# A fused attention and feed-forward kernel on one core: the pooled weights' product on both row halves, a new planned order, and more matmuls ahead of the first transpose

## The chip, the cores and the metric

The kernel runs on 1 core of one Trainium2 chip. The metric is the device time of one execution in microseconds; lower is better. The kernel before took 918.63 us, the median of 3 runs (918.45 to 920.07).

Names of the engines: PE (TensorE, matmuls), DVE (VectorE), ACT (ScalarE), POOL (GpSimd) and SP, whose queue issues nearly all the transfers. PEld is PE's loading of weights.

## The reference, cut to what matters

```
q, k, v: 8 batches x 8 heads x 576 rows x 64         (fp32)
pooled:  rows averaged in fours -> 144 rows; softmax(q4 k4^T / 8) v4; each result row repeated 4 times
local:   softmax of q k^T / 8 where |i - j| < 4, times v
x = (pooled + local) as 4608 tokens x 512
h = x @ w_in                       (512 x 2048)
g = h * clip(h + 3, 0, 6) / 6
out = g @ w_out                    (2048 x 512)
```

All of it is fp32. The two large products are made of three matmuls each on values split in a high and a low part (hi*hi, hi*lo, lo*hi).

## The kernel before, in words

**Feed-forward.** The 4608 tokens are 9 chunks of 512 (PART). A chunk has 16 steps f. Step f of the first product (`gemm1`, line 1031) is 12 matmuls of 128x512 into PSUM bank h0 or h1. Then ACT makes relu(h+3) (line 1037), DVE min(.,6)*h (line 1041), ACT the high part (line 1045), and DVE or POOL the low part (line 1049). Step f of the second product (`gemm2`, line 1081) is 12 matmuls into the four banks o0 to o3, one for each 128 tokens. All in all that is 2 x 1728 matmuls of this kind.

**Attention.** A unit is two heads of one batch, 32 units in all. The first 8 units (`alone`, batches 0 and 1) have their steps planned one by one: q and k are transposed by PE (line 385, batch 0), masks (699) and local scores (707), pooled scores (504), softmax on DVE, ACT and POOL, transposes of the probabilities (597, 732), and the products with v (`pv_d` 678, `pv` 750). The other 24 units go in bursts: one PE operation holds the pooled scores of a new unit (`scores_d4`, 521), the products of an older unit (`pv`, 750, and `pv_d4`, 666), and the local scores of the new one (707). A burst works in banks h0 and h1. The transposed probabilities of these units come by way of DRAM (`put_d`, `get_d`, `put`, `get`).

**The pooled product of a burst.** `pv_d4` multiplies 144 pooled probabilities by the pooled v. 128 of the 144 rows are on 128 partitions, two row halves of 64. The last 16 rows of the two heads are 32 partitions of the lower row half. So there are three passes: row half 0, row half 1, and row half 0 once more for the rest, with 144 columns each and two heads side by side.

**Weights.** Each block of `w_in` or `w_out` comes as 64-bit numbers and is made into two fp32 parts: ACT (line 185), "low" on ACT or DVE (198, 200), "bits" on DVE (190), "hi" on ACT or DVE (119, 121: a helper, `copy_on`) and "lo" on POOL or DVE (210).

**What sets the order.** The program makes a list of operations with a cost each, what they depend on, the buffers they take and a due time. `Plan.emit` walks through time with these costs and picks for each free engine the operation that is due first. T0, TC, TF and FIRST are due times, COST and PEN the costs and preferences where more than one engine can do an operation, `dma` and `Queue` the model of the transfers. An operation with `lock` on DVE or POOL is not put beside another one of that kind on the other of the two. While PE has nothing to do before the first gemm, `busy` (line 1133) puts matmuls on the identity between its operations. The result is a fixed list of instructions for each engine; on the chip each engine works through its own list in order and waits only for its operands.

## Time and profile before

| | |
|---|---|
| median of 3 runs | 918.63 us (918.45 to 920.07) |
| profiled execution, own time | 915.05 us |
| its span, first to last instruction | 913.2 us |
| PE busy | 899.2 us (98%), 7002 matmuls |
| DVE, ACT, POOL busy | 530.9 us (58%), 430.1 us (47%), 230.2 us (25%) |
| mean granted TensorE clock | 0.999 |
| moved by DMA | 93.41 MB, 102 GB/s over the span |

The profiled execution was 3.58 us shorter than the median of the runs, and its span 1.85 us shorter than its own time. A matmul's recorded time overlaps with that of the next one, so the pace of PE is read from the starts of its rows, not from a mean. In a row of the order of time the columns are: start in us, length in us, engine, line, operation, result and operand, tile of the array or shapes, number of instructions, and in brackets the idle time before it with what ended it.

### The profile page before, as it was taken

Reading aid. Unit: us, or ns where it says so; the run is one execution under the profiler, and the core shown is the slowest. Engines: PE = TensorE matmul, PEld = TensorE weight load, DVE = VectorE, ACT = ScalarE, POOL = GpSimd, SP = SyncE. Lnnn points to the kernel's source line nnn. Section 1 sums busy time; section 2 is a strip of 40 time slices with the busy share of each in tenths; the row PEclk is TensorE's granted clock in tenths of the full one; section 3 lists DMA queues with packets and bytes.
Section 4 is the critical chain, followed back from the end, with each engine's and each line's share of the span. In section 5 each row is a group of like instructions: output and inputs, shape, how many; then the busy total and the mean of one; then the engine's idle time right before and its main releaser. Section 6 shows DMA issues by size and latency. Waiting matters only on the chain.

```text
span 913.2 us, 19160 instructions
## 1 busy us (share of the span) xinstructions
PE 899.2 (98%) x7002; PEld 730.9 (80%) x7002; DVE 530.9 (58%) x965; ACT 430.1 (47%) x1438; POOL 230.2 (25%) x316
## 2 busy tenths in 40 slices
PE   8899999999999999999999999999999999999997
PEld 6577778788888888888888888888888888888886
DVE  7989866676755567556745675556654432233222
ACT  5977745566554555345535564455542222222221
POOL 5685532222322231223212330225000000010000
PEclk9999999999999999999999999999999999999999
DMA  9989433666736456355644555555522010001001
GB/s 251 290 231 293 100 82 77 128 120 134 146 85 128 100 112 144 78 104 106 139 97 93 114 116 126 105 104 105 134 59 48 1 47 1 1 1 46 1 1 46
DMA packets 311565, 93.41 MB, mean 102 GB/s; under 512 B 250800, under 2 KB 296880, under 8 KB 311472
## 3 DMA queue, kind: packets, MB, share of 16 engines
q1 hardware_dynamic: 310800, 91.29, 44.4%
q8 instruction: 55, 0.90, 0.4%
q10 hardware_dynamic: 672, 0.91, 0.3%
q14 instruction: 38, 0.31, 0.1%
HBM read 69.53 MB, written 22.61 MB: 101 GB/s over the span
## 4 chain that ended last, share of the span: by engine, by line
PE 91%; DVE 3%; DMA 2%; ACT 1%; SPq 1%; issue 1%; POOL 0%; ACTq 0%; DVEq 0%
PE h L1031 42%; PE o L1081 41%; PE a L707 2%; PE h L750 1%; PE h L666 1%; PE a L521 1%; DMA arena<-in_k_dram 1%; ACT arena L571 1%; DMA out_dram<-arena 0%; DMA pd<-arena 0%; PE a L504 0%; PE a L678 0%; SPq L985 0%; DMA arena<-in_v_dram 0%; PE a L750 0%
## 5 line engine op out<-in xcount | busy, mean ns | idle before, releaser
L1081 PE MATMUL o<-wp,rounded 128*128 128x512 f32 x1728 | 414.4, 392 | 0.0
L1031 PE MATMUL h<-rounded,wp 128*128 128x512 f32 x1728 | 407.8, 391 | 2.0 <-DVE first L755 1.4
L1031 PEld LDWEIGHTS h<-rounded,wp 128*128 128x128 f32 x1728 | 322.6, 188 | 72.0 <-issue 2.8
L1081 PEld LDWEIGHTS o<-wp,rounded 128*128 128x128 f32 x1728 | 321.2, 188 | 69.4 <-issue 0.8
L1041 DVE SCALAR_TENSOR_TENSOR arena<-arena,h 128x512 f32<-128x512 f32 x144 | 97.8, 679 | 127.1 <-ACT arena L1037 126.8
L1037 ACT ACTIVATE arena<-h 128x512 f32<-128x512 f32 x144 | 85.7, 595 | 181.7 <-PE h L1031 180.8
L1045 ACT CAST rounded<-arena 128x512 fp32r<-128x512 f32 x144 | 88.8, 617 | 112.1 <-DVE arena L1041 61.9
L1049 DVE TENSOR_TENSOR rounded<-arena,rounded 128x512 fp32r<-128x512 f32 x105 | 72.4, 692 | 101.5 <-PE o L1081 96.6
L1049 POOL TENSOR_TENSOR rounded<-arena,rounded 128x512 fp32r<-128x512 f32 x39 | 51.9, 1333 | 168.5 <-PE o L1081 88.7
L377 DVE STREAM_TRANSPOSE arena<-arena 128x576 f32<-128x576 f32 x56 | 43.3, 775 | 67.3 <-DMA arena<-in_q_dram 34.1
L571 ACT ACTIVATE arena<-arena 128x64 f32<-128x64 f32 x240 | 80.1, 336 | 0.2
L571 ACT ACTIVATION_READ_ACCUMULATOR arena<-arena 128x1 f32 x240 | 45.3, 189 | 0.0
L453 POOL TENSOR_TENSOR arena<-arena 32x256 f32<-32x256 f32 (+1 forms) x26 | 19.4, 746 | 94.4 <-DMA arena<-in_v_dram 90.7
L547 ACT ACTIVATE arena<-arena 128x1 f32<-128x1 f32 (+1 forms) x78 | 15.0, 192 | 47.6 <-DVE arena L560 47.6
L454 POOL TENSOR_TENSOR arena<-arena 32x128 f32<-32x128 f32 (+1 forms) x26 | 12.8, 494 | 96.9 <-PE h L666 95.7
L682 ACT ACTIVATE arena<-h 128x144 f32<-128x144 f32 x24 | 7.0, 290 | 63.7 <-PE h L666 63.7
L451 DVE TENSOR_REDUCE arena<-arena 128x128 f32<-128x512 f32 (+1 forms) x26 | 27.6, 1061 | 13.4 <-PE h L666 9.2
L934 POOL TENSOR_TENSOR rounded<-arena,rounded 128x768 fp32r<-128x768 f32 (+3 forms) x5 | 8.9, 1789 | 98.4 <-ACT rounded L119 94.8
L415 POOL TENSOR_TENSOR arena<-arena 128x144 f32<-128x144 f32 x52 | 31.8, 612 | 4.1
L588 DVE TENSOR_TENSOR arena<-arena 128x432 f32<-128x432 f32 (+1 forms) x42 | 29.8, 710 | 1.4
L633 DVE STREAM_TRANSPOSE arena<-arena 128x384 f32<-128x384 f32 (+1 forms) x48 | 22.2, 467 | 13.5 <-DMA arena<-pd 13.0
L707 PE MATMUL a<-arena 64*64 64x64 f32 x1160 | 28.7, 224 | 0.0
(192 smaller groups left out, 783.9 us busy)
## 6 DMA issues: line engine op xcount, KB each, us to landing
arena<-in_v_dram SPq DMA_DIRECT2D x58, 160.0 KB
rawp<-in_w_in_dram SPq DMA_DIRECT2D x16, 512.0 KB
rawp<-in_w_out_dram SPq DMA_DIRECT2D x16, 512.0 KB
arena<-in_q_dram SPq DMA_DIRECT2D x112, 72.0 KB
arena<-in_k_dram SPq DMA_DIRECT2D x112, 72.0 KB
pl<-arena SPq DMA_DIRECT2D x24, 320.0 KB
arena<-pl SPq DMA_DIRECT2D x96, 80.0 KB
arena<-in_v_dram SPq DMA_DIRECT2D x28, 256.0 KB
```

The lines of the kernel that those rows point to most:

```text
L377: nc.vector.transpose(out=qk[kind], in_=qk[kind])
L415: eng.tensor_tensor(t, t, x[:, :, r], op=ALU.add)
L451: eng.tensor_reduce(out=vd, in_=raw.rearrange("p r e -> p e r"), op=ALU.add, axis=AX.X)
L571: nc.scalar.activation(x[:, j], x[:, j], AF.Exp, bias=m[:, j:j + 1], scale=0.125, accum_out=s[:, j:j + 1])
L588: eng.tensor_tensor(x, x, s.unsqueeze(2).broadcast_to(list(x.shape)), op=ALU.mult)
L707: nc.tensor.matmul(st["ps", g][half:half + WIN, jj * D:jj * D + WIN], qk_of("q")[hs, k_first:k_first + WIN], qk_of("k")[hs, k_first:k_firs ...
L1031: nc.tensor.matmul(st["ps"], win[f][:, wt, kk * P:(kk + 1) * P], xs[part][:, kk], start=(kk == 0 and i == 0), stop=(kk == NK - 1 and i == ...
L1037: nc.scalar.activation(st["t"], st["ps"], AF.Relu, bias=3.0)
L1041: nc.vector.scalar_tensor_tensor(out=t, in0=t, scalar=6.0, in1=st["ps"], op0=ALU.min, op1=ALU.mult)
L1045: nc.scalar.copy(st["gh"], st["t"])
L1049: eng.tensor_tensor(st["gl"], st["t"], st["gh"].bitcast(F32), op=ALU.subtract)
L1081: nc.tensor.matmul(otile[n, m], gt[:, ms], wout[f][:, wt], start=(f == 0 and i == 0), stop=(f == NF - 1 and i == 2),)
```

## The change

- `pv_d4`: the last 16 rows of both heads are put on both row halves of the array, on partitions 0 to 31 and 64 to 95. Row half 0 then makes the first 24 of the 48 query columns of each group, and row half 1 the last 24. `ld4`, `sum4`, `get_d` and `turn_d` put the operands there: four small loads of v in place of two, one more memset, and transposes and multiplications of 96 partitions in place of 32.
- The planner's numbers: due times (T0 from 55.0 to 44.6, FIRST, LAGW, a list SHIFT of one offset for each unit), costs of transfers (`dma`, LAND, SLOW, LATE), costs and preferences of engines (COST, PEN), a doubled PE cost before COLD = 5.9, and a rule (`sooner`) by which an operation waits for another engine that would finish it earlier.
- The high part of g (`ghi`) may be made by DVE as well as by ACT. It, the split of x (`xhi`) and, where it is not done by way of a PSUM bank, the "hi" of the weights are locked against POOL.
- More matmuls on the identity are put ahead of the first transpose, by another rule in `fetch`.
- The last chunk: steps f = 14 of two of the four banks are done ahead of f = 15, each bank is evicted by one engine (ACT or DVE) in place of two halves one after the other, and the stores are dealt to SP and ACT by size.

```
@@ pv_d4
-            for g in (0, 1, 2):
-                ks = slice(g % 2 * D, (g % 2 + 1) * D)
+            for g in range(2):
+                ks = slice(g * D, (g + 1) * D)
                 for h in range(2):
                     hs = slice(h * D, (h + 1) * D)
                     nc.tensor.matmul(
-                        st["pod"][g % 2][hs].rearrange("p (j q) -> p j q", j=3), st["vd"][ks, g // 2, hs],
-                        used(st["pdt"][ks], h * D, 2 * D) if g < 2 else used(st["pdt"][ks], 6 * D, D),
-                        start=(g < 2), stop=(g > 0), skip_group_check=True)
+                        st["pod"][g][hs].rearrange("p (j q) -> p j q", j=3), st["vd"][ks, 0, hs],
+                        used(st["pdt"][ks], *((3 * h * D, D) if apart else (h * D, 2 * D))), start=True, stop=False,
+                        skip_group_check=True)
+            for g in range(2):
+                ks, q = slice(g * D, (g + 1) * D), QB // 2
+                x = st["pdt"][ks]
+                for h in range(2):
+                    hs = slice(h * D, (h + 1) * D)
+                    nc.tensor.matmul(
+                        st["pod"][g][hs].rearrange("p (j q) -> p j q", j=3)[:, :, g * q:(g + 1) * q], st["vd"][ks, 1, hs],
+                        bass.AP(tensor=x.tensor, offset=x.offset + 6 * D + g * NAR, ap=[x.ap[0], [D, 3], [1, q]]),
+                        start=False, stop=True, skip_group_check=True)
@@ ld4
-                for h in range(2):
-                    nc.sync.dma_start(
-                        raw[h * KR:(h + 1) * KR], src(v_all, row0 + 4 * P, [[4 * ROW, KR], [1, 4 * ROW]]))
+                for first in (0, KR, D, D + KR):
+                    nc.sync.dma_start(raw[first:first + KR], src(v_all, row0 + 4 * P, [[4 * ROW, KR], [1, 4 * ROW]]))
@@ sum4
-                eng.memset(st["vd"][NAR:D, 1], 0.0)
+                for i in range(2):
+                    eng.memset(st["vd"][i * D + NAR:(i + 1) * D, 1], 0.0)
@@ turn_d
-            n, a, e = (P, 0, 12 * NAR) if i == 0 else (NAR, 12 * NAR, 18 * NAR)
+            n, a, e = (P, 0, 12 * NAR) if i == 0 else (D + NAR, 12 * NAR, 18 * NAR)
@@ plan_weights, plan_split, plan_moe
-        e = op(on("whi", cols), 0, hi, [d])
+        e = op(on("whi", cols), 0, hi, [d], lock=not by_bank)
...
-                       free=free, dl=start_of(n) - 1.0)
+                       free=free, dl=start_of(n) - 1.0, lock=True)
...
-            d = op("ACT", 0.17 + size / 1130, hi, [c], take=[("gh" + k0, ("gh", key))])
+            d = op(on("ghi", size), 0, hi, [c], take=[("gh" + k0, ("gh", key))], lock=True)
@@ plan_store (last chunk)
-            e = [op("ACT", 0.37, partial(ev_half, 0, nc.scalar), [ready], take=[("obz", (n, m))], free=[frees])]
-            e.append(op("DVE", 0.37, partial(ev_half, 1, nc.vector), [ready] + e, take=[("obz", (n, m))], free=[frees]))
+            e = [op("ACT" if m % 2 == 0 else "DVE", (0.60, 0.69)[m % 2], partial(ev_last, nc.scalar if m % 2 == 0 else nc.vector), [ready],
+                    take=[("obz", (n, m))], free=[frees])]
@@ numbers
-T0, TC, TF, LAG = 55.0, 82.0, 5.1, 2
+T0, TC, TF, LAG = 44.6, 82.0, 5.1, 2
-FIRST = 16.0, 8.0
+FIRST = 7.5, 4.1
-    "whi": {"ACT": (0.12, 1 / 1200), "DVE": (0.1, 1 / 960)},
+    "whi": {"ACT": (0.12, 1 / 1200), "DVE": (0.09, 1 / 1800)},
+    "ghi": {"ACT": (0.17, 1 / 1130), "DVE": (0.09, 1 / 1800)},
-    return Load(packets * (7.8 + 0.0446 * size if size > 256 else 10.8 + 0.0375 * size) / 16e3, packets / 16)
+    return Load(packets * (18.0 + 0.045 * size if size > 256 else 10.8 + 0.0375 * size) / 16e3, packets / 16)
@@ fetch
-            self.idle = self.warm.start + 1.2
+            self.idle = self.warm.start + 0.4
...
-            gap = (t - self.idle - IDLE[1]) * (IDLE[2] if t > 8.0 else 0.5 * IDLE[2])
-            o.busy = max(0, int(gap / IDLE[0]))
+            one = IDLE[0] if t > COLD else 2 * IDLE[0]
+            gap = (t - self.idle - IDLE[1]) * (IDLE[2] if t > COLD else 1.0)
+            o.busy = max(0, int(gap / one))
```

Three places of the order. The first is PE's list at its very start; `identb` is the identity, `h` the bank the fill writes, `a` and `o` banks that take transposes, scores follow. Before, 3 matmuls on the identity stand ahead of the first transpose:

```order
L1133 MATMUL h_114<-identb 128x512
L385 MATMUL a_118<-ident,arena 128x128 x4
L385 MATMUL a_125<-ident,arena 128x128 x4
L385 MATMUL o_132<-ident,arena 128x128
L385 MATMUL o_134<-ident,arena 128x128
L385 MATMUL o_145<-ident,arena 128x128 x4
L699 LDWEIGHTS identb
L699 MATMUL o_153<-maskb,identb 128x320
```

and now 14, with one more before the second unit's transposes:

```order
L1151 MATMUL h_117<-identb 128x512
L387 MATMUL a_132<-ident,arena 128x128 x4
L387 MATMUL a_139<-ident,arena 128x128 x4
L387 MATMUL o_146<-ident,arena 128x128
L387 MATMUL o_148<-ident,arena 128x128
L1151 LDWEIGHTS identb
L1151 MATMUL h_117<-identb 128x512
L387 MATMUL o_158<-ident,arena 128x128 x4
L710 LDWEIGHTS identb
L710 MATMUL o_164<-maskb,identb 128x320
```

What follows is in the same order; only the fill is longer.

The second place is DVE's list up to the sum of the two attention parts of the fourth unit (`first` is x, 288 and 224 its columns; `rawp` and `wp` are weights, `early<-a`/`o` evictions). Before:

```order
L409 TENSOR_REDUCE arena<-arena 128x144
L190 SCALAR_TENSOR_TENSOR o_642<-o_642,rawp_386 128x512
L121 COPY arena<-a_511 16x128
L755 TENSOR_TENSOR first<-o_389,arena 128x64
L121 COPY early<-a_665 128x256
L200 TENSOR_SCALAR rawp_580<-rawp_580 128x512
L210 TENSOR_TENSOR wp_673<-o_642,wp_673 128x512
L755 TENSOR_TENSOR first<-o_548,early 128x64
L190 SCALAR_TENSOR_TENSOR early<-rawp_383 128x512
L190 SCALAR_TENSOR_TENSOR early<-rawp_412 128x512
L755 TENSOR_TENSOR first<-o_696,early 128x288
L755 TENSOR_TENSOR first<-a_697,early 128x224
```

and now:

```order
L121 COPY early<-a_619 16x3x2x48
L121 CAST rounded<-first 128x224
L121 COPY early<-o_633 128x256
L211 TENSOR_TENSOR wp_617<-o_581,wp_617 128x512
L379 STREAM_TRANSPOSE arena<-arena 128x576
L191 SCALAR_TENSOR_TENSOR early<-rawp_488 128x512
L379 STREAM_TRANSPOSE arena<-arena 128x576
L766 TENSOR_TENSOR first<-o_666,early 128x288
L766 TENSOR_TENSOR first<-o_667,early 128x224
```

From the first maximum of a softmax to this sum DVE has 70 instructions before and 62 now: six evictions from PSUM and three weight operations ("bits" twice, "lo" once) less, one "low" of weights and one sum of four rows of v more. Three scalings of 432 columns that ACT did in three instructions each (line 586) are now on POOL.

The third place is PE at the change from chunk 0 to chunk 1: `pv` of the eighth unit (L750, now L761), `gemm2` of the last steps of chunk 0 (`wp_1574` is step 14 and `wp_1628` step 15 before, `wp_1711` step 15 now), the first burst (L521 and on, now L523) and `gemm1` of chunk 1. Before:

```order
L750 MATMUL a_1777<-arena 64x61 x2
L1081 MATMUL o_872<-wp_1574,rounded 128x512 x3
L1081 MATMUL o_891<-wp_1574,rounded 128x512 x3
L1081 MATMUL o_899<-wp_1574,rounded 128x512 x3
L1081 MATMUL o_911<-wp_1574,rounded 128x512 x3
L521 MATMUL a_1820<-arena 64x144 x2
...
L1081 MATMUL o_872<-wp_1628,rounded 128x512 x3
L1031 MATMUL h_1865<-rounded,wp_540 128x512 x12
```

and now:

```order
L761 MATMUL a_1807<-arena 64x61 x2
L1096 MATMUL o_845<-wp_1711,rounded 128x512 x3
L1096 MATMUL o_860<-wp_1711,rounded 128x512 x3
L523 MATMUL a_1844<-arena 64x144 x2
...
L1046 MATMUL h_1886<-rounded,wp_617 128x512 x12
```

Between the last product of the eighth unit and the first matmuls of chunk 1 there were 15 matmuls of 128x512 and the short burst; now there are 6 and the burst.

More of the change, by code (lines that the diff above doesn't have):

```diff
@@ L485, in plan_unit @@
             rk = "raw" + k0, ("v", un, g)
-            l = op("SP", 0.5, partial(ld4, g), take=[rk], size=dma(P, 512) if alone and g else dma((P, NAR)[g], 2048), nd=1 if alone else 1 + g)
+            l = op("SP", 0.5, partial(ld4, g), take=[rk], size=dma(P, 512) if alone and g else dma((P, 2 * NAR)[g], 2048), nd=1 if alone else 1 + 3 * g)
             if alone and g:
@@ L694, in scores @@
         def scores():
-            if alone:
+            if apart:
                 places()
-            for g in range(2 if alone else 0):
+            for g in range(2 if apart else 0):
                 nc.tensor.matmul(
@@ L780, in scores_l, with pv_all @@
             scores()
-        def pv_all(hb):
-            st["px"] = hb
+        def pv_all(hb=None):
+            st["px"] = hb or [bank(PS, ("x", un, g)) for g in range(2)]
             pv()
@@ L1092, in plan_moe @@
             if n == len(PART) - 1 and f == NF - 2:
+                for m in range(parts // 2):
+                    prev.append(op("PE", cost, partial(g, m), after + prev[-1:], dl=dl, rec=3))
                 continue
@@ L1194 @@
 LAGT = 0.5
-LAGW = 2.0
+LAGW = 0.5
 SUMMED = 0, 1, 2, 3
@@ L1438, in emit @@
         since = {}
+        every = list({slot: None for l in self.slots.values() for slot in l})
+        clash = {slot: [x for x in every if overlap(slot, x)] for slot in every}
         turn = {key: [] for key in ORDERED}
+        rings = {key: key[:-1] if key.endswith("1") and key[:-1] in turn else key for o in self.ops for key, _ in o.take}
         def ring(key):
-            return key[:-1] if key.endswith("1") and key[:-1] in turn else key
+            return rings[key]
         for o in self.ops:
@@ L1448, in emit, with room @@
                     turn[ring(key)].append((key, h))
+        stamp = [0]
         def fits(o, without=()):
+            if not o.take:
+                return []
+            if not without and o.tried == stamp[0]:
+                return None
+            got = room(o, without)
+            if got is None and not without:
+                o.tried = stamp[0]
+            return got
+        def room(o, without):
             got = []
@@ L1457, in fits @@
                 for slot in sorted(self.slots[key], key=lambda x: since.get(x, 0.0)):
-                    if not any(overlap(slot, x) for x in list(holder) + [x for _, x in got]):
+                    if not any(x in holder for x in clash[slot]) and not any(x in clash[slot] for _, x in got):
                         got.append(((key, h), slot))
@@ L1463, in fits, with sooner @@
             return got
+        def sooner(e, o):
+            mine = t + o.on[e][0]
+            for other, (cost, later) in o.on.items():
+                start = max(engine_free[other], t) + cost + MARGIN
+                if other == e or start > mine:
+                    continue
+                key = o.late + later
+                start += sum(x.on[other][0] * (0.5 if x.choice else 1.0) for late, _, x in ready[other] if late < key and x is not o)
+                if start < mine:
+                    return True
+            return False
         self.left, self.block, self.idle = FETCH[1], 0.0, None
```

160 lines of the change are left out of this document (96 added, 64 removed), and 4 rows, old and new, of the table SHIFT.

## The prediction

> **What bounds the kernel now.** I read the page's busy shares first, then a table of PE's work by stage (columns: stretch and its length in us; for PE, PEld, DVE, ACT and POOL busy us with the number of instructions; then clock, DMA share, GB/s), then the chain of waits, whose longest pieces are all like the last row here.
>
> ```profile
> PE 899.2 (98%) x7002; PEld 730.9 (80%) x7002; DVE 530.9 (58%) x965; ACT 430.1 (47%) x1438; POOL 230.2 (25%) x316
> 717.63 5.44 PE h L1031 x24
> ```
>
> ```profile
> 4.72:9.68 4.96, 4.96 (x56) 4.26 (x57) 2.89 (x4) 1.06 (x3) 1.57 (x3) 1.00 1.04 341
> 9.68:32.92 23.24, 22.02 (x388) 15.20 (x384) 22.50 (x55) 20.27 (x70) 17.73 (x27) 1.00 1.04 232
> 32.92:45.38 12.46, 10.65 (x136) 7.18 (x132) 11.63 (x27) 10.63 (x25) 7.20 (x10) 1.00 1.00 355
> 78.92:83.73 4.81, 3.66 (x25) 2.72 (x19) 4.81 (x8) 2.52 (x4) 1.96 (x2) 1.00 1.03 411
> 176.78:194.87 18.09, 16.81 (x76) 13.35 (x73) 12.59 (x25) 9.93 (x44) 5.86 (x10) 1.00 0.66 125
> 194.87:694.04 499.17, 498.98 (x4289) 412.82 (x4288) 307.00 (x585) 253.24 (x1002) 129.87 (x198) 1.00 0.53 110
> 694.04:907.68 213.64, 213.64 (x989) 176.48 (x988) 69.01 (x102) 50.04 (x84) 6.03 (x6) 1.00 0.06 15
> ```
>
> There are two regimes. From about 45 us on PE is the bound: 24 matmuls take 5.44 us, 0.2267 us each, so the 3456 large ones need 783.4 us of the 913.2, and between 45.38 and 907.68 PE has only two idle places of weight, 4.81 - 3.66 = 1.15 us and 18.09 - 16.81 = 1.28 us; with the 0.19 us of the long stretch 2.62 us in all. There a change is worth what it takes off PE, and nothing else. Before 45 us DVE is the bound: 22.50 of 23.24 us and 11.63 of 12.46. What counts there is when the first chunk's x is complete, since all large matmuls wait for it.
>
> **1. The pooled product of a burst.** The same shapes stand in the burst's own pooled scores: 144 columns on all four quarters of the array (8 instructions), then 72 columns on all four (8 instructions); and the pooled product stands at the end of a single product.
>
> ```profile
> 571.76 0.48 PE L521 MATMUL a<-arena 64*64 64x144 f32 x8
> 572.06 0.31 PE L521 MATMUL h<-arena 64*64 64x72 f32 x8
> 572.18 0.63 PE L750 MATMUL h<-arena 64*64 64x60 f32 x31
> 693.45 0.67 PE L666 MATMUL h<-arena 64*64 64x144 f32 x12
> 694.04 0.50 PE L1081 MATMUL o<-wp,rounded 128*128 128x512 f32 x1
> ```
>
> By the starts, the 72 columns cost 572.18 - 572.06 = 0.12 us and the 144 columns 572.06 - 571.76 = 0.30, with the start-up of the burst in it. The 12 instructions of `pv_d4` take 694.04 - 693.45 = 0.59 us with the switch to the large matmuls: two passes of 144 columns side by side and one alone, the third as long as the first two together, since its 144 columns use only one row half; about 0.25 us each. The third becomes 72 columns on both halves, 0.12. That is 0.12 us less in each of 24 units: **-2.9 us**. It lies on PE where PE is the bound. Bounds: at least half, -1.4, should the freed row half have been used by the local scores that follow in the burst; at most 0.13 x 24 = -3.1.
>
> What it adds is off the path. Two more issues of v for each unit and one more memset:
>
> ```profile
> L442 SPq DMA_DIRECT2D arena<-in_v_dram x48: 322/413/637, 129.3 to 675.4; - x48
> L459 POOL MEMSET arena<- 32x128 f32 x23 | 4.5, 196 | 0.9
> POOL arena L453: 90.7, 20
> ```
>
> 2 x 0.413 = 0.83 us of SP's queue and 0.196 us of POOL. Behind them in SP's list stand the next loads of q, k and v. Who waits for this load is POOL (the last row: 90.7 us in 20 waits), which is busy 129.87 of 499.17 us and early for each unit. Cost 0; without that cover 24 x 1.0 us of lateness would reach PE only where a unit has no slack, a few us.
>
> **2. The fill ahead of the first transpose.**
>
> ```profile
> 1.66 1.46 PE L1133 MATMUL h<-identb 128*128 128x512 bf16 x3 [1.66 <-DVE identb L138]
> 4.72 1.94 PE L385 MATMUL a<-ident,arena 128*128 128x128 f32 x8 [1.60 <-DMA arena<-in_k_dram]
> 6.45 1.49 PE L385 MATMUL o<-ident,arena 128*128 128x128 f32 x6
> 15.23 1.20 PE L385 MATMUL o<-ident,rows 128*128 128x128 f32 x9
> 16.27 0.27 PE L385 MATMUL a<-ident,rows 128*128 128x128 f32 x1
> ```
>
> The first eight transposes take (6.45 - 4.72)/8 = 0.216 us each, later ones (16.27 - 15.23)/9 = 0.116. So everything from 4.72 to about 9.68 ran at half pace, although the column of the granted clock says 1.00: 4.96 us of work that needs 2.5. The fill is 14 matmuls now. At the pace of the three, about 0.41 us (the third starts at some 2.49), they last until 1.66 + 14 x 0.41 = 7.4 us, while k has landed by 4.72. So the fill is longer than the wait that it covers. If PE has its full pace at 7.4, the first unit's scores end at 7.4 + 2.5 = 9.9 us instead of 9.68; if the pace doubles half way, about 9.3; if it never comes before them, 12.4. I take **+0.5 us** for DVE's first softmax step (bounds -0.4 and +2.7).
>
> The Trainium skill, "TensorE: Matmul & The Clock Gate", Part 1, says that the slow phase is about 3.4 us of sustained activity, by a window that runs freely, and not a number of matmuls. By that rule the pace would double between about 5 and 8.5 us, in other executions at other times, and the step would come out between -0.4 and +1.3. The row of 4.72 to 9.68 fits it: 4.96 us until the pace doubled.
>
> **3. The first 45 us.** DVE is the bound there, so its list decides. Up to the last sum of x of the fourth unit:
>
> ```profile
> 11.90 0.69 DVE L121 COPY arena<-a 128x512 f32<-128x512 f32 x1
> 37.33 0.67 DVE L210 TENSOR_TENSOR wp<-o,wp 128x512 fp32r<-128x512 f32 x1
> 38.06 1.27 DVE L190 SCALAR_TENSOR_TENSOR early<-rawp 128x512 int32<-128x512 int32 x2
> 39.63 0.37 DVE L755 TENSOR_TENSOR first<-a,early 128x224 f32<-128x224 f32 x1
> ```
>
> Start to start an instruction is some 0.08 us shorter than its length: "lo" 0.60, two "bits" 1.20, a copy of 512 columns 0.61, one of 256 columns 0.33. The change takes off DVE before this point two "bits" (1.2), one "lo" (0.6), six copies (about 2.1) and 0.4 us of a cast, and adds one "low" (0.33) and one sum of v (1.0): 3.0 us of about 28.7. It starts 0.5 later by step 2, so the sum moves from 39.9 to about 37.5: **-2.4 us**. ACT loses three scalings by column and gains evictions, and was busy 20.27 of 23.24: near, but not over. Bounds: 0, if ACT or POOL takes over as the bound, and -4.0, if DVE's 1.6 us of waits in the two stretches go as well. After 45 us PE does the same work as before, so what is won here lasts to the end if weights and DVE keep pace.
>
> **4. Waits of PE later on.** The two places above, 1.15 and 1.28 us, have the same kind of cause, a list that came too late (DVE at 79, a transfer to DRAM at 176). A new order removes these and may make others. I take half, **-1.2 us** (bounds -2.6 and +2.0). One new place I can name: at the change to chunk 1 only 6 large matmuls and a short burst stand between the last product and `gemm1`, where there were 15.
>
> ```profile
> 143.71 0.81 PE L750 MATMUL a<-arena 64*64 64x60 f32 x40
> 144.55 0.82 DVE L755 TENSOR_TENSOR arena<-a,arena 128x288 f32<-128x288 f32 x2 [1.71 <-PE a L750]
> 146.07 1.09 DVE L934 TENSOR_TENSOR rounded<-arena,rounded 128x896 fp32r<-128x896 f32 x1
> 147.41 0.48 PE L521 MATMUL a<-arena 64*64 64x144 f32 x8
> 148.52 0.97 PE L1081 MATMUL o<-wp,rounded 128*128 128x512 f32 x3
> ```
>
> From the product's end (about 144.45) to the split's end (147.16) are 2.7 us, plus 0.2 to PE. In that time PE has 6 x 0.2267 = 1.4 us, a burst of 148.52 - 147.41 = 1.1, and the switch, 0.2. So some **+0.3 us** (0 to +1.0).
>
> **5. The end.**
>
> ```profile
> 908.61 0.38 ACT L996 ACTIVATE arena<-o 128x256 f32<-128x256 f32 x1 [1.48 <-DMA out_dram<-arena]
> 909.02 0.42 DVE L998 TENSOR_SCALAR arena<-o 128x256 f32<-128x256 f32 x1 [1.44 <-DMA out_dram<-arena]
> 909.48 0.87 ACTq L1002 DMA_DIRECT2D out_dram<-arena  x2
> ```
>
> The last bank's eviction began late, behind ACT's own issue of stores (the bracket of the first row), and was done at 909.44. Now DVE alone evicts it; its 512 columns at 0.69 us from about 908.1 end at 908.8, and SP and ACT issue two stores each behind it. SP's queue is a little longer then. **-0.5 us** (-1.0 to 0).
>
> **The sum.** -2.9 - 2.4 - 1.2 + 0.3 - 0.5 = -6.7 us. Against the profile: span 913.2 - 6.7 = 906.5, own time 915.05 - 6.7 = 908.4. The median of the runs is 3.58 us over the profiled execution, so 912.0.
>
> **The rivals.** (a) *The start gives nothing* (0.18): the long fill costs what DVE saves, or ACT becomes the bound. Then -6.7 + 2.4 = -4.3, with a unit more of fill -3.3: 914 to 915.5, take 915. For it: the fill's own arithmetic. Against: DVE at 97% of that stretch.
>
> (b) *All waits vanish* (0.10): -3.1 - 4.0 - 2.6 - 1.0 = -10.7, 908.
>
> (c) *DVE slows down where it is full* (0.09), the case on the other side. DVE and POOL disturb each other:
>
> ```profile
> L121 DVE CAST wp<-arena 128x512 fp32r<-128x512 f32 x3 | 1.3, 417 | 0.1
> L121 DVE CAST rounded<-first 128x512 fp32r<-128x512 f32 x1 | 1.1, 1127 | 0.5 <-PE h L1031 0.5
> L200 DVE TENSOR_SCALAR rawp<-rawp 128x1024 int32<-128x1024 int32 x5 | 7.0, 1392 | 0.0
> 75.95 0.65 DVE L200 TENSOR_SCALAR rawp<-rawp 128x1024 int32<-128x1024 int32 x1
> 63.81 2.17 DVE L200 TENSOR_SCALAR rawp<-rawp 128x1024 int32<-128x1024 int32 x1
> 60.00:80.00 20.00, 20.00 (x133) 15.31 (x132) 19.22 (x21) 14.16 (x26) 14.69 (x10) 1.00 0.97 251
> ```
>
> The same cast takes 417 or 1127 ns and the same "low" 0.65 or 2.17 us. The new order gives DVE 16 "low" in place of 8, not locked against POOL: 7 of 1024 and 9 of 512 columns. All slowed, the seven cost 7 x 1.52 = 10.6 us more and the nine, taken at half of that, 6.8; the eight of before paid already 5 x (1.39 - 0.65) = 3.7 and about 0.8. That is up to +13 us on DVE at a time when it is full 19.22 of 20. At three quarters, +9.8 - 6.7 = +3.1: 922. It decides from half on. Against: four "lo" fewer on DVE there, and the casts are locked.
>
> The Trainium skill, "SBUF — State Buffer", section "Who interferes with whom", says that a copy, cast or tensor_scalar in a two-port mode and a GpSimd instruction exclude each other for the whole instruction. By it each collision would cost DVE the rest of a POOL instruction, which is this rival; the two lengths of the same cast agree with it.
>
> (d) *The new order waits more in the long stretch* (0.08): five waits of the size at 176 (1.28 us) eat all: 918.5, no change.
>
> **How the numbers follow.** My case has 0.55 and its own range is 908.5 to 915.5 (the bounds of steps 3 and 4 moved one at a time). With (a) and (b) inside, and the rest of (c) and (d) outside, 8 of 10 lie in 907 to 917.5. What differs by less than 0.2% (916.8 to 920.5) is about what a measurement of this kernel cannot tell from no change. Faster: 0.55 + 0.16 of (a) + 0.10 + 0.02 of (c) and (d) = 0.83; no change: 0.02 of (a) and 0.07 of (d) = 0.09; slower 0.08.
>
> **What would show it.** Step 1: the starts between the pooled product's two halves, 0.12 us, and a burst of 2.06 instead of 2.18 us. Step 2: the start of the first transpose near 7 us, and the pace of the ones behind it. Step 3: the last sum of x of the fourth unit near 37.5 us, and the first unbroken run of large matmuls 2 us earlier. Step 4: PE's idle time from 45 us on under 2.6 us, and a wait of some 0.3 us at the head of chunk 1. Step 5: the last store's issue half a us nearer to the last matmul. I am wrong if DVE's "low" run long between 40 and 110 us and PE waits for weights, or if PE's idle time in the long stretch is several us.

## The result, and the profile after

The changed kernel takes 906.64 us, the median of 4 runs (906.03 to 908.61), and the kernel before 919.35 beside it (918.45 to 921.37). The ratio is 0.9862, 95% interval 0.9839 to 0.9886: 1.4% faster, 12.7 us, where -6.7 us was forecast. The time lies just under the predicted range (907.0 to 917.5). The profiled execution has an own time of 906.03 us and a span of 904.2. Between the two profiles the span fell by 9.0 us. The other 3.7 us come from the distance between a kernel's profiled execution and the median of its runs: 919.35 - 915.05 = 4.3 us before, 906.64 - 906.03 = 0.6 us now.

The table of stages of the changed kernel, with the same columns as the one of before (stretch and its length; busy us and instructions of PE, PEld, DVE, ACT and POOL; clock, DMA share, GB/s), ahead of it the page's line of PE:

```profile
PE 895.5 (99%) x7112; PEld 729.1 (81%) x7112; DVE 566.1 (63%) x1040; ACT 390.6 (43%) x1363; POOL 241.0 (27%) x332
9.68:33.83 24.15, 22.88 (x397) 15.82 (x396) 24.12 (x57) 19.67 (x70) 19.37 (x28) 1.00 0.98 207
33.83:43.21 9.38, 8.96 (x121) 6.48 (x119) 8.75 (x20) 6.07 (x18) 6.20 (x9) 1.00 1.02 349
43.21:147.39 104.18, 104.18 (x820) 80.59 (x820) 91.43 (x131) 64.29 (x124) 57.64 (x46) 1.00 0.67 178
147.39:694.00 546.61, 546.61 (x4703) 452.64 (x4703) 360.77 (x702) 261.35 (x1086) 150.39 (x231) 1.00 0.54 112
694.00:898.49 204.49, 204.49 (x1004) 168.96 (x1002) 76.88 (x123) 36.29 (x65) 4.28 (x7) 1.00 0.07 18
```

DVE is still the bound before the long run (24.12 of 24.15 us). The stretch from the first large matmul to the 25th, which was 32.92 to 45.38, is 33.83 to 43.21: 3.1 us shorter. From 43.21 to 898.49 PE is busy in every hundredth that the table can show; both places of 1.15 and 1.28 us are gone.

The order of time at the start, for PE and then for DVE (start, length, engine, line, operation, number, and in brackets the idle time before):

```profile
1.66 4.76 PE L1151 MATMUL h<-identb 128*128 128x512 bf16 x14 [1.66 <-DVE identb L138]
6.26 1.04 PE L387 MATMUL a<-ident,arena 128*128 128x128 f32 x8
9.57 0.48 DVE L562 TENSOR_REDUCE arena<-o 128x5 f32<-128x320 f32 x1
35.15 0.76 DVE L379 STREAM_TRANSPOSE arena<-arena 128x576 f32<-128x576 f32 x1
35.84 0.70 DVE L766 TENSOR_TENSOR first<-o,early 128x288 f32<-128x288 f32 x2
```

The 14 matmuls of the fill last until 6.26, not 7.4, since the pace doubled within them; the eight transposes behind them take 7.13 - 6.26 = 0.87 us instead of 1.73. The scores are done near 9.2 us, but a reduction on DVE (8.90 to 9.65 us) stands ahead of the first softmax step. The last sums of x of the fourth unit (L766) end at 36.5 instead of 40.0 us.

A burst, and the change to chunk 1:

```profile
582.65 0.48 PE L523 MATMUL a<-arena 64*64 64x144 f32 x8
583.65 0.43 PE L668 MATMUL h<-arena 64*64 64x144 f32 x8
583.90 0.30 PE L677 MATMUL h<-arena 64*64 64x72 f32 x8
584.72 0.50 PE L1096 MATMUL o<-wp,rounded 128*128 128x512 f32 x1
144.61 1.67 PE L1096 MATMUL o<-wp,rounded 128*128 128x512 f32 x6
146.30 1.09 DVE L950 TENSOR_TENSOR rounded<-arena,rounded 128x896 fp32r<-128x896 f32 x1
147.39 1.89 PE L1046 MATMUL h<-rounded,wp 128*128 128x512 f32 x7
```

The burst is 584.72 - 582.65 = 2.07 us (before, from 571.76 to 573.94, 2.18). At the change to chunk 1 the split ends at 147.39, just when PE comes to it.

What DVE waits for ahead of the transposes of q and k of the later units, before and after (us in total, times, longest):

```profile
DVE arena L377 <- DMA arena<-in_q_dram: 34.1, 19, 4.2
DVE arena L377 <- DMA arena<-in_k_dram: 32.0, 23, 2.4
```

```profile
DVE arena L379 <- DMA arena<-in_k_dram: 3.0, 4, 1.8
DVE arena L379 <- DMA arena<-in_q_dram: 1.7, 1, 1.7
```

The prediction did not use this view, since DVE is not the bound behind 45 us. 42 of 56 transposes of before stood waiting for a load, 66.1 us in all, and now 5, 4.7 us.

### The profile page after: what moved, and what is told of

The parts are those of the page before. It is cut to its first block, busy times and chain, and to the rows that moved or that the text cites. A ratio compares the mean times of both kernels' runs of the same rounds, so it can differ in the third digit from the quotient of the medians.

```text
span 904.2 us, 19563 instructions
## 1 busy us (share of the span) xinstructions
PE 895.5 (99%) x7112; PEld 729.1 (81%) x7112; DVE 566.1 (63%) x1040; ACT 390.6 (43%) x1363; POOL 241.0 (27%) x332
## 4 chain that ended last, share of the span: by engine, by line
PE 96%; DVE 2%; ACT 1%; issue 0%; POOL 0%; POOLq 0%; DVEq 0%
PE o L1096 44%; PE h L1046 43%; PE a L718 2%; PE h L761 2%; PE a L523 1%; PE h L668 1%; PE h L1151 1%; PE a L689 0%; PE a L506 0%; DVE rawp L201 0%; PE a L761 0%; PE h L677 0%; PE h L523 0%; PE a L743 0%; PE a L599 0%
## 5 line engine op out<-in xcount | busy, mean ns | idle before, releaser
L1064 POOL TENSOR_TENSOR rounded<-arena,rounded 128x512 fp32r<-128x512 f32 x46 | 62.4, 1357 | 169.3 <-PE o L1096 106.5
L119 ACT CAST rounded<-arena 128x512 fp32r<-128x512 f32 (+2 forms) x79 | 49.7, 629 | 101.0 <-PE o L1096 80.8
L121 DVE CAST rounded<-arena 128x512 fp32r<-128x512 f32 (+4 forms) x81 | 36.3, 450 | 4.9 <-PE h L1046 1.0
L452 DVE TENSOR_REDUCE arena<-arena 128x128 f32<-128x512 f32 (+1 forms) x28 | 30.1, 1075 | 13.8 <-PE h L668 7.9
L415 POOL TENSOR_TENSOR arena<-arena 128x144 f32<-128x144 f32 x28 | 13.9, 495 | 89.7 <-PE h L523 30.1
L454 POOL TENSOR_TENSOR arena<-arena 96x256 f32<-96x256 f32 (+1 forms) x24 | 19.5, 812 | 62.9 <-DMA arena<-in_v_dram 46.8
L417 POOL TENSOR_TENSOR arena<-arena 128x144 f32<-128x144 f32 x56 | 32.8, 585 | 4.4
L455 POOL TENSOR_TENSOR arena<-arena 96x128 f32<-96x128 f32 (+1 forms) x24 | 11.1, 464 | 76.4 <-PE h L677 73.7
L211 POOL TENSOR_TENSOR wp<-early,wp 128x1024 fp32r<-128x1024 f32 (+1 forms) x12 | 27.2, 2268 | 14.3 <-ACT wp L119 12.3
```

What stands on the lines that cost most here:

```text
L119: nc.scalar.copy(out_, in_)
L121: eng.tensor_copy(out_, in_)
L417: eng.tensor_tensor(t, t, x[:, :, r], op=ALU.add)
L452: eng.tensor_reduce(out=vd, in_=raw.rearrange("p r e -> p e r"), op=ALU.add, axis=AX.X)
L1064: eng.tensor_tensor(st["gl"], st["t"], st["gh"].bitcast(F32), op=ALU.subtract)
```

## Experiments

Labels with b_ start from the kernel before, those with a_ from the changed kernel.

### 1. Before once more: is its profile an ordinary execution?

No edit.

> The kernel before, unchanged, profiled and timed again. The span of its first profiled execution was 913.2 us (own time 915.05), while its timed executions took 918.45 to 921.37. Theory 1 (more waiting inside the span): ordinary executions have spans of 916.5 to 919.5 us, own time and span keep their distance of 1.85 us, and a profile of one of them shows 3.5 to 6 us more of idle time of PE between the 1728 + 1728 large matmuls than the first profile's (2.6 us after 45 us). Theory 2 (a difference outside the span): spans stay near 913 us and the own time is 5 to 8 us over the span. Theory 3 (scatter of the start): the extra time lies before 45 us, as a later first gemm.

> The kernel before once more, one profile. Theory 1: where its own time is 918 us or more, PE's idle places between 45 us and the last matmul add up to 5 to 9 us, at the same places as in the other profile of this kernel (a fixed weakness of the order: transfers or DVE that come just in time). Rival: at other places each time (chance, for instance a refresh or a stray transfer). Theory 2: span near 913 us and no more idle time.

b_again: 918.15 us in the median of 10 (915.35 to 921.9), profile 916.54 with a span of 914.7. b_again2: 919.70, span 917.8. Own time and span keep a distance of 1.85 to 1.9 us in each profile, so theory 2 falls. The first profile (915.05) was an exception: of 86 timed executions of this kernel in the whole study one, 914.14, was faster. The rows of the first profile, of b_again and of b_again2 at one place, the transposition of k on DVE and the PE transposes behind the sum that comes after it:

```profile
33.75 0.78 DVE L377 STREAM_TRANSPOSE arena<-arena 128x576 f32<-128x576 f32 x1 [1.05 <-POOL rounded L934]
35.02 0.52 PE L732 MATMUL a<-ident,early 128*128 128x128 f32 x3 [1.13 <-DVE first L755]
```

```profile
34.58 0.78 DVE L377 STREAM_TRANSPOSE arena<-arena 128x576 f32<-128x576 f32 x1 [1.70 <-POOL rounded L934]
35.84 0.52 PE L732 MATMUL a<-ident,early 128*128 128x128 f32 x3 [1.78 <-DVE first L755]
PE h L1031 <- DVE first L755: 2.8, 2, 2.0
PE o L1081 <- DVE rounded L1049: 0.8, 1, 0.8
```

```profile
34.97 0.78 DVE L377 STREAM_TRANSPOSE arena<-arena 128x576 f32<-128x576 f32 x1 [2.12 <-DMA arena<-in_k_dram]
36.24 0.52 PE L732 MATMUL a<-ident,early 128*128 128x128 f32 x3 [2.20 <-DVE first L755]
PE h L1031 <- DVE first L755: 2.0, 2, 1.6
PE o L1081 <- DVE rounded L1049: 1.4, 1, 1.4
```

The load of k lands at 33.7 (or before), 34.6 or 35.0 us. DVE's list has its transposition ahead of the sum of x that PE waits for, so PE's wait follows it: 1.13, 1.78, 2.20 us. (The third row names the load. The POOL instruction in the first two brackets can't be what ended the second wait: it must be over by 33.75 in the first profile, and stands only 0.2 us later in b_again. In the first profile either can be it.) The other rows are of the views of PE's waits. The two waits of L1031 are at 181 us (1.3 us in the first profile, 0.8 in b_again, 1.6 in b_again2) and at 235 us (0.2, 2.0, 0.4); that of L1081 is at 636 us (0, 0.8, 1.4). Two of the longer ones follow a load on DVE's list too, at 235 us in b_again one of v and at 636 us in b_again2 one of k, with the low part of g (L1049) that PE waits for behind it:

```profile
233.37 1.03 DVE L451 TENSOR_REDUCE arena<-arena 128x128 f32<-128x512 f32 x1 [1.50 <-DMA arena<-in_v_dram]
639.44 0.78 DVE L377 STREAM_TRANSPOSE arena<-arena 128x576 f32<-128x576 f32 x1 [3.08 <-DMA arena<-in_k_dram]
640.14 1.79 DVE L1049 TENSOR_TENSOR rounded<-arena,rounded 128x512 fp32r<-128x512 f32 x2
```

By the starts of the large matmuls b_again loses 1.84 us on the first profile at 235 and 0.87 at 636, b_again2 0.29 and 1.45. At the 25th large matmul they are already 0.83 and 2.88 us behind. But where the first profile waits itself, they gain: b_again 1.5 us at 84 us and 0.5 at 181, b_again2 1.0 at 84. At the last large matmul they are 1.44 and 4.57 us behind. So theory 1 holds for the places, and theory 3 for a part: fixed weak places, with another length each time.

### 2. Does the half pace behind the wait cost the time?

In b_again2 the granted clock fell behind the wait of 2.20 us. The table of the stretches 36 to 39, 39 to 42 and 42 to 46 us (the clock is the third number from the end):

```profile
36.00:39.00 3.00, 2.76 (x12) 1.73 (x12) 2.49 (x8) 2.78 (x6) 2.80 (x5) 0.61 1.01 388
39.00:42.00 3.00, 3.00 (x52) 2.54 (x54) 2.17 (x5) 1.64 (x4) 0.71 (x1) 0.50 1.09 324
42.00:46.00 4.00, 4.00 (x30) 3.23 (x24) 3.41 (x11) 3.58 (x11) 1.38 (x2) 0.81 1.02 406
```

```diff
+        on_pe = [o for o in order if o.eng == "PE"]
+        on_pe[43].busy = 5        # 5 matmuls on the identity ahead of the transposes at 35 us
```

> The kernel before with 5 more matmuls on the identity between its first three large matmuls and the transposes at 35 us, where PE waited 1.13, 1.78 and 2.20 us in three profiles and where, behind the longest of these, the granted clock was 0.61 and 0.50 for 6 us. 5 x 0.2267 = 1.13 us of the wait is filled, and nothing on its path is later. Theory (half pace is the result of a long idle place of PE): no execution has a granted clock under 0.998, where 5 of 10 had 0.995 or 0.996; the slow half of the times, 918.7 to 921.9, is gone, and the median is 916 to 917. Rival (the clock falls for another reason): clocks of 0.995 and 0.996 in a third or a half of the executions as before, median 918.4.

The first half held: in none of 10 executions the mean clock was under 0.998. The second fell: 918.07 us, ratio to before 1.0012 (0.9994 to 1.0030), and times up to 923.0 are still there. The half pace is real, but what it costs here can't be told from nothing. b_again2 was 3.95 us behind the first profile at 43 us, 2.77 at 68 and 1.57 at 85, where the first profile has its own wait of 1.15 us. That PE's pace costs nothing here because DVE bounds this stretch is argued, not shown.

### 3. The product and the fill, undone one at a time

```diff
 pv_d4 (a_oldpv; get_d and turn_d put the operands as before)
-            for g in range(2): ... 144 columns on each row half, then 72 columns on each
+            for g in (0, 1, 2): ... 144 columns on row half 0, on 1, and on 0 once more
 emit (a_fill3)
-                busy(o.busy)
+                busy(min(o.busy, 3))
```

> The changed kernel with the pooled product in three passes again (and the transposed probabilities where these passes need them); the order of all other work is the changed kernel's. Theory (the third pass at 144 columns costs PE 0.12 us more in each of 24 bursts): 2.8 us slower than the changed kernel, so about 909.5 us, a burst of 2.18 us instead of 2.06. Rival (the product's time is hidden behind the local scores of the other row half): same time as the changed kernel, 906.6, burst 2.06.

> The changed kernel with 3 matmuls of fill instead of 14 ahead of the first transpose; the order of all else is unchanged. Theory (it is the time since the first matmul that ends the half pace, and DVE bounds the start): first transpose at 4.7 us at half pace, pace doubles between 5 and 9.7 us; DVE's first softmax step near 9.6 to 9.8 us, so the whole is 0 to 0.3 us slower than the changed kernel (906.6 to 906.9). Rival (the fill is what wins the start, because all scores then run at full pace): first softmax step at 10.5 us or later and the whole 1 us or more slower, 907.6 or more.

a_oldpv: 908.86 us, ratio 0.9886 (0.9872 to 0.9901); that is 2.2 us over the changed kernel. In the two profiles the start of the last large matmul moves from 898.49 to 901.36, 2.87 us, and it grows burst by burst. The product is worth what was predicted. a_fill3: 906.29, ratio 0.9863 (0.9844 to 0.9882): no difference. Its first large matmul starts at 34.21 instead of 33.83, its last at 898.68 instead of 898.49. The 11 more matmuls cost nothing and bring 0.2 us at most, although DVE's first softmax step starts at 10.09 us without them and at 9.57 with them.

### 4. The model of the transfers, alone and undone

```diff
-    return Load(packets * (7.8 + 0.0446 * size if size > 256 else ...
+    return Load(packets * (18.0 + 0.045 * size if size > 256 else ...
-ISSUE, LAND = 0.5, (1.8, 1.3, 25.0)
+ISSUE, LAND = 0.55, (1.8, 1.3, 25.0, 4.8)
+SLOW, LATE = 1.09, 0.7
```

> The kernel before with the changed kernel's model of the transfers alone (packet cost, landing time not before 4.8 us, factor 1.09, 0.7 us later, 0.55 us an issue); all due times, preferences and the pooled product as before. Theory A (the model of the transfers takes DVE's waits away): DVE waits for q and k ahead of its transposes under 20 us in all, where the kernel before has 66 us in 42 waits; PE's waits from 30 us on under 2 us, the granted clock 0.999 or 1.000 in each execution, 3 to 4 us faster than before's median of 918.35: 914 to 915.5. Rival B (the due times do it): DVE's waits stay over 45 us and the time within 1.5 us of 918.35.

> The changed kernel with the old model of the transfers alone; due times, list of offsets for each unit and preferences stay the changed kernel's. Theory A: DVE's waits for q and k come back, from 5 us to over 40 us, PE waits 2 us or more from 30 us on in ordinary executions, 909 to 913 instead of 906.6. Rival B (the due times and offsets do it): waits of DVE for q and k stay under 15 us, 906.5 to 908.

b_dma has this edit alone: 916.92 us, ratio 0.9995 (0.9978 to 1.0011). DVE's waits for q and k fell from 66 to 13.5 us, as theory A said, and 8 of 10 executions lie between 915.4 and 917.6, but the time did not follow. Its waits of PE:

```profile
PE o L1081 <- ACT arena L979: 1.5, 5, 0.3
PE h L1031 <- DVE arena L1041: 1.3, 1, 1.3
PE o L1081 <- DVE wp L210: 0.9, 1, 0.9
```

Other waits have taken the place of the old ones: from 10 us on PE's waits of this view are 6.0 us in all, where the first profile of before has 4.9, b_again 6.9 and the changed kernel 1.6. a_olddma takes the edit back out of the changed kernel: 925.66 us, ratio 1.0094 (1.0072 to 1.0116), 19 us over the changed kernel and slower than before. DVE waits 31.7 us for q and k there, and PE up to 2.5 us at a time behind DVE's steps of gemm1. Theory A's direction held, but its size did not, and neither theory foresaw that the new model would be worth nothing without the other numbers.

### 5. Later loads on purpose

Each load of q or k of the later units as six transfers instead of four, in the order as it is:

```diff
-            for e in range(4):                                   # 32 partitions, 18 blocks
+            for e, first, n in ((0, 0, 9), (0, 9, 9), (1, 0, 9), (1, 9, 9), (2, 0, 18), (3, 0, 18)):
```

> The kernel before, in the same order, with each load of q or k of the later units issued as six transfers instead of four (the same bytes and packets): two more issues at some 0.41 us each, so each such load lands about 0.8 us later, the second of a pair 1.7 us. Theory (the order before has loads that land just in time, and DVE's list stands still behind them): DVE's waits for q and k go from 66 us to over 90, PE's waits from 30 us on grow by 3 us or more, and the time goes from about 918 to 921 to 926. Rival (such waits are covered): within 1 us of 918.

> The changed kernel, in the same order, with the same six transfers in place of four. Theory (the new order has 1 to 2 us of room ahead of each of these loads): DVE's waits for q and k grow from 5 us to 10 to 30, PE's waits stay under 2 us, and the time stays under 908 (906.6 without). Rival (both orders are as sensitive): 3 us or more slower, 909.6 or more.

b_split: 944.78 us, ratio 1.0273 (1.0232 to 1.0314), 26.8 us slower than before. a_split: 914.5 us, ratio to before 0.9958 (0.9941 to 0.9975), 7.9 us slower than the changed kernel. DVE's waits in the two:

```profile
DVE arena L377 <- DMA arena<-in_k_dram: 64.0, 26, 5.0
DVE arena L377 <- DMA arena<-in_q_dram: 52.4, 20, 5.6
```

```profile
DVE arena L379 <- DMA arena<-in_k_dram: 19.9, 15, 4.0
DVE arena L379 <- DMA arena<-in_q_dram: 15.0, 11, 3.1
```

The theory held for before, by more than it said. For the new order its numbers fell (under 908 was expected): the room is less than the lateness, 0.8 to 1.7 us by the estimate above. The edit delays what stands behind these loads in SP's list as well: in a_split DVE waits 6.4 us for loads of v, where the changed kernel has 1.9, so q and k alone are not singled out. What stands is the size: the same edit costs the old order some three times as much. A part of that is half pace: the mean granted clock of b_split's four executions was 0.989 to 0.995, and 0.999 or 1.000 in a_split. In the profile (943.8 us at 0.989) that is some 21 us at half pace, so up to 10 us of the loss, by an estimate.

### 6. The other numbers, undone one at a time

```diff
a_shift0    SHIFT = [0.0] * 32
a_nosooner  -                    if o.choice and sooner(e, o):
            -                        continue
a_oldT0     T0 = 55.0 (44.6); FIRST = 16.0, 8.0 (7.5, 4.1)
a_oldpen    PEN of the kernel before; "ghi": {"DVE": 5.0}
a_ghiact    -            d = op(on("ghi", size), 0, hi, [c], ..., lock=True)
            +            d = op("ACT", 0.17 + size / 1130, partial(hi, nc.scalar), [c], ...)
```

> The changed kernel with all offsets of the units' due times at zero; transfers' model, preferences and product stay. Theory A (the model of the transfers takes the waits away, the offsets only polish): 907 to 910. Rival B (only all numbers together make an order without waits; alone, each is worth nothing): 912 or more, with PE's waits of 4 us or more from 30 us on.

> The changed kernel without the rule by which an operation waits for another engine that would finish it sooner. Rival B (only all numbers together make an order without waits): 909 or more, with PE's waits of 3 us or more. Theory A (the rule is one of many, the transfers' model carries the order): 906 to 908.5.

> The changed kernel with the old due times of the first gemm and of the first weights (T0 55.0 instead of 44.6, FIRST 16.0 and 8.0 instead of 7.5 and 4.1). Theory A (these due times are what brings the first unbroken run of large matmuls forward): the last sum of x of the fourth unit at 38.5 to 40 us instead of 36.5, the 24th large matmul at 45 to 46 us instead of 43.2, and 909 to 911. Rival B (they only have to fit the list of offsets): the start as in the changed kernel within 0.7 us, and the time is lost later, in PE's waits behind 46 us. Rival C (they do nothing): 906 to 907.5.

> The changed kernel with the old preferences between engines (PEN; the high part of g counted as the other casts, 5.0). Theory (the preferences take DVE's and ACT's late steps of gemm1 away from PE): PE's waits from 30 us on go from under 1.5 us to 4 us or more, 910 to 915. Rival (preferences only shuffle work between engines that have time): 906 to 908.

> The changed kernel with the high part of g on ACT alone again. Theory (DVE as a second place for it takes ACT's lateness away): PE waits for ACT or for DVE behind ACT 2 us or more from 46 us on, 908 to 912. Rival (ACT has time, busy about 45% after 46 us): 906 to 907.5.

| undone | median us | ratio to before | over the changed kernel's 906.64 |
|---|---|---|---|
| offsets (a_shift0) | 911.71 | 0.9927 (0.9901 to 0.9954) | +5.1 |
| the rule (a_nosooner) | 906.22 | 0.9866 (0.9836 to 0.9896) | -0.4 |
| T0, FIRST (a_oldT0) | 914.08 | 0.9951 (0.9931 to 0.9971) | +7.4 |
| preferences (a_oldpen) | 909.94 | 0.9919 (0.9894 to 0.9944) | +3.3 |
| "hi" of g on DVE (a_ghiact) | 908.11 | 0.9903 (0.9875 to 0.9931) | +1.5 |

The changed kernel was not run again beside these, and the kernel before took 918.0 us beside them instead of 919.35; by the ratios each amount of the table is 0.8 to 2.3 us larger. So the amounts are good to some 2 us. The rule shows no effect, as theory A said; the offsets lie between the two theories, and the preferences just under their theory's range. T0 and FIRST do more than theory A said, and elsewhere: up to the 25th large matmul a_oldT0 is 1.7 us later than the changed kernel, but the loss is made between 49 and 69 us, and behind that it keeps about 9 us up to the end. Its rows there, of the orders of time on DVE and PE, and the clock in the table of stretches:

```profile
51.86 2.86 DVE L201 TENSOR_SCALAR rawp<-rawp 128x1024 int32<-128x1024 int32 x1
56.53 0.68 DVE L211 TENSOR_TENSOR wp<-o,wp 128x512 fp32r<-128x512 f32 x1
57.27 1.65 PE L1096 MATMUL o<-wp,rounded 128*128 128x512 f32 x3 [3.81 <-DVE wp L211]
56.00:60.00 4.00, 2.73 (x9) 2.34 (x10) 4.00 (x6) 2.13 (x4) 0.24 (x1) 0.52 0.89 142
60.00:64.00 4.00, 4.00 (x12) 3.12 (x12) 1.52 (x3) 2.90 (x5) 0.21 (x1) 0.63 1.00 296
```

A block of weights comes too late: its "low" takes 2.86 us on DVE, where one took 0.65 in the kernel before. It starts 0.25 us behind the start of a "lo" on POOL (51.61 to 54.16 us) and ends 0.56 us behind that one's end. PE waits 3.81 us for the weights, and the starts of its matmuls are at half pace behind the wait, up to about 62.8 us, here on its own bound. This is rival (c) of the prediction and the half pace together. In the changed kernel the "low" are long as well, but their weights come early enough:

```profile
L201 DVE TENSOR_SCALAR rawp<-rawp 128x1024 int32<-128x1024 int32 x7 | 10.6, 1520 | 0.0
L201 DVE TENSOR_SCALAR rawp<-rawp 128x512 int32<-128x512 int32 x9 | 6.2, 694 | 0.0
60.00:80.00 20.00, 20.00 (x109) 16.06 (x100) 19.73 (x23) 11.11 (x23) 14.46 (x13) 1.00 1.00 304
```

By the starts of the large matmuls a_oldpen has all of its loss by 58 us and a_ghiact most of it between 166 and 251 us; a_shift0 has half by 73 us and the rest later, in steps of up to 1.4 us. The amounts of the edits undone sum to some 38 us (with the product 2.2 and the transfers 19.0) where all together are worth 12.7: each fits the others.

### 7. The end

```diff
a_oldend  ACT and DVE evict half a bank each, stores dealt in turn (as before)
a_end3    stores dealt to SP, ACT and POOL: every[0::3], every[1::3], every[2::3]
a_banks   -                for m in range(parts // 2):       # step 14 of two banks ahead of step 15
          +                for m in range(0):
          -                    both = m >= parts // 2
          +                    both = True
```

> The changed kernel with the old eviction and stores of the last chunk (each bank in two halves, ACT and then DVE; stores dealt in turn). Between the last large matmul's start and the end of the span the changed kernel has 5.7 us and the kernel before 5.5. Theory (the long part is a store's own time behind its issue, so the eviction's half us does not show): 5.4 to 5.8 us again, and a time within 0.3 us of the changed kernel. Rival (the new end is worth what was predicted, 0.5 us, and something else took it): 6.2 us.

> The changed kernel with the last chunk's stores dealt to three queues, SP, ACT and POOL, in place of SP and ACT. In the changed kernel SP issues its last 10 stores without a pause from 896.14 to 901.65 us, ACT its last at 900.73, and the span ends 2.6 us behind SP's last. Theory (SP's backlog sets the end): SP has 6 or 7 stores and is done near 900.5 us, so the end lies 4.6 to 5.0 us behind the start of the last large matmul instead of 5.7, and the time is about 0.9 us under the changed kernel, 905.7. Rival (the last transfers' own time, or POOL's slower issue, sets it): 5.5 us or more, and no gain.

> The changed kernel with one difference in the last 24 large matmuls: step 15 of the first bank comes directly behind its step 14, as in the kernel before, so this bank is complete 3 matmuls (0.68 us) earlier, 18 matmuls ahead of the end instead of 15. The shorter eviction stays. In the changed kernel the stores of the last chunk, 1.05 MB, move at 150 to 215 GB/s without a pause from 896.9 to 902.7 us. Theory (these transfers bound the end, so the first bank's completion sets it): from the last large matmul's start to the end 5.0 to 5.4 us instead of 5.75, and a time 0.3 to 0.7 us under the changed kernel, about 906.1. Rival (the last bank's own chain sets it): 5.7 us again, and 906.6.

From the start of the last large matmul to the end of the span: before 5.50 us, the changed kernel 5.75, a_oldend 5.62 (907.24 us, one run), a_end3 5.83 (907.80), a_banks 5.01 (905.85; 905.41 to 906.64; ratio 0.9863, 0.9836 to 0.9890). These are single profiles, and the end differs from one to the next. Nine other versions have the changed kernel's list of instructions in the last chunk (a_oldpv, a_split, a_shift0, a_oldpen, a_oldT0, a_olddma, a_fill3, a_nosooner, a_ghiact), and their ends are 5.24, 5.26, 5.29, 5.38, 5.47, 5.64, 5.64, 5.76 and 5.79 us; with the changed kernel's own the mean is 5.52. The kernel before has 5.50, 5.54 and 5.58. So the new end neither wins nor loses anything that can be seen, and a_oldend's 5.62 says the same of the eviction; its time is no sign, since its first large matmul already starts 1.2 us later. In a_end3 SP is done with its issues 1.0 us earlier and the end stays, so SP's queue does not set it. Only a_banks lies outside, 0.5 us under the mean and 0.23 under the lowest. That points at when the transfers of the last chunk begin, but one profile does not show it. The rows of the changed kernel, then of a_banks, at the first and the last of these transfers (the last number is GB/s):

```profile
896.00:897.00 1.00, 1.00 (x6) 0.84 (x5) 0.69 (x1) 0.11 (x1) 0.00 (x0) 1.00 0.09 23
902.00:903.00 1.00, 0.00 (x0) 0.00 (x0) 0.00 (x0) 0.00 (x0) 0.00 (x0) 0.79 0.28 88
```

```profile
896.00:897.00 1.00, 1.00 (x7) 0.79 (x5) 0.69 (x1) 0.00 (x0) 0.00 (x0) 1.00 0.54 143
902.00:903.60 1.60, 0.00 (x0) 0.00 (x0) 0.00 (x0) 0.00 (x0) 0.00 (x0) 0.77 0.01 5
```

Between these rows the stores move at 135 to 217 GB/s in both kernels, in stretches of 1 us. With the first bank 0.68 us earlier the end came 0.74 us earlier than in the changed kernel's profile, and 0.5 earlier than in the mean of the ten. a_banks has the lowest median and the shortest end here, though its time can't be told from the changed kernel's by 4 runs.

## Why the prediction was wrong in size

The direction and most mechanisms were right; 912.0 was 5.4 us too high.

**The step that failed is the last one of the sum: "the median of the runs is 3.58 us over the profiled execution, so 912.0".** It carries the distance over as if it were a constant of the machine. Experiment 1 shows what much of it was: waits of PE at fixed places, most of them behind loads that come just in time, which were shorter in the first profile than in the ordinary executions; that profile was a lucky case. The changed kernel's distance is 906.64 - 906.03 = 0.6 us; 3.0 of the 5.4 us lie here. The spread of the times stood in the text (918.45 to 920.07 against 915.05), and 42 waits of DVE on loads stood in the trace.

The other 2.3 us are the profiles' own difference, -9.0 against -6.7, and there the term that was mis-sized most is step 4:

- *Step 1, product, -2.9:* right. 2.07 against 2.18 us a burst, the 72 columns of L677 stand where 144 stood; undone, +2.87 us in the profile and +2.2 in the median.
- *Step 2, fill, +0.5:* wrong in sign, within its bounds. DVE's first softmax step starts at 9.57 instead of 9.78 us: -0.2, and DVE's own reduction held it, not the scores. The pace doubled inside the fill, at about 4.9 us, so the fill ended at 6.26. The Trainium skill, "TensorE: Matmul & The Clock Gate", Part 1, gives about 3.4 us of activity for this; from 1.66 to 4.9 us agrees.
- *Step 3, the first 45 us, -2.4:* right in kind, mis-sized. The last sum of x ends 3.5 us earlier (40.0 to 36.5), of which 1.05 is DVE's wait at 33, that the step had only in its bound. The 25th large matmul starts 2.2 us earlier (45.38 to 43.21).
- *Step 4, later waits, half of 2.62, and +0.3 at chunk 1:* mis-sized. All of them went, and more than the busy column showed. From the 25th large matmul to the last one the time fell by 7.0 us, of which the product is 2.7; 4.3 are waits. No wait appeared at chunk 1. I took half for want of a reason. That DVE would no longer wait for loads would have been one to take more, though b_dma shows that this alone does not do it.
- *Step 5, the end, -0.5:* wrong. The two profiles differ by +0.25, and the ends of ten executions have a mean of 5.52 us where before has 5.50 to 5.58: nothing was won. The step priced the last bank's eviction. What sets the end is open; a_banks points at the first bank's completion, which the change put 0.68 us closer to the end (experiment 7).

Of the rivals, (b), all waits vanish, 908, is nearest, with a chance of 0.10. Its number is near by luck in part: PE's later waits did vanish, but its terms for the start (-4.0) and the end (-1.0) did not come in full, and the distance of 3.58 us, which it kept, made up for them. (a) did not: DVE's savings came through, and the fill cost nothing. (c) was half right: the "low" on DVE are slow, 1.52 us in the mean, and DVE is full, 19.73 of 20 us, but PE does not wait; with the old due times it does (a_oldT0). (d) did not come.

What is not settled: why the numbers of the plan work only together. Each edit undone shows its loss at other places, and no single one, nor the model of the transfers alone, makes the gain. How late a load can be before the new order loses time was not measured; it is less than the 0.8 to 1.7 us (by an estimate) of experiment 5. What sets the end of the kernel is open as well.

## What to carry to other kernels

Compare the profiled execution's own time with the timed runs before anything else: where it is faster than all of them, the ordinary executions may hold waits that it does not show, and a change of order can remove them, as here, so the distance belongs in the bounds and not in the sum as a constant. Where lists are fixed, count the instructions that stand waiting for a transfer on every engine, even one that is half idle: behind each of them the list stands still, and its lateness differs from execution to execution. A due time, a preference or a cost in a plan that was tuned together can't be priced alone.

## What the hardware showed that was not expected

- The granted clock falls to half behind a wait of PE of 2.20 us (0.61, 0.50 and 0.81 in three stretches from 36 to 46 us) and of 3.81 us (0.52 and 0.63 in two stretches from 56 to 64 us), while no drop followed the ones of 1.78 and 2.00 us in b_again (mean clock 1.000). The Trainium skill, "TensorE: Matmul & The Clock Gate", Part 1, speaks of an idle window of about 3.4 us for this; here 2.20 us was enough. In the start's slow phase, in contrast, the column reads 1.00 although the pace is half.
- Two more issues in each load of q and k, some 0.8 us a load by an estimate, cost 26.8 us in an order that waits for them in 42 places, and 7.9 us in one that waits in 5.
- By the start of DVE's step behind it, one load landed at least 1.2 us apart in three executions of the same program (33.7 to 35.0 us), and PE's wait behind it was 1.1 us apart. In the latest of the three SP had begun to issue it 0.8 us later (27.84 instead of 27.05 us); in b_again only 0.07 us later, with the landing 0.8 us later.
